# Ones beside the values: one 128-column product for values and denominators in a fused attention and feed-forward kernel

## Chip, cores, metric

One core of one Trainium2 chip. The metric is the device time of one execution in microseconds, lower is better.

## The reference, cut

```python
def _attn_ref(q, k, v):                      # 8 batches, 8 heads, 576 tokens, 64 columns
    scores = np.matmul(q, k.transpose(0, 1, 3, 2)) / sqrt(64)
    mask = np.abs(pos[:, None] - pos[None, :]) <= 32
    scores = np.where(mask, scores, -1e9)
    attn = np.exp(scores - max)
    attn = attn / (np.sum(attn, axis=-1, keepdims=True) + 1e-09)
    return np.matmul(attn, v)

x = attn_out.transpose(0, 2, 1, 3).reshape(4608, 512)
h = x @ w_in                                 # 512 -> 2048
g = 0.5 * h * (1 + tanh(c * (h + 0.044715 * h**3)))
out = g @ w_out                              # 2048 -> 512
```

## The kernel before

A turn of the main loop handles 512 tokens: 112 products of 256 columns of the second layer (a seven-product scheme for 2 x 2 blocks), and between them, by a plan, the attention of the next batch; then the first layer of the next 512 tokens. Heads go in pairs. For a pair `g` the steps are `s` (scores and their exponential), `m` (mask), `v` (weigh, and invert the sums) and `x` (spread: multiply and store into the ring `xT`). `-1` means the tails of the batch before.

```python
PLAN = {6: "s0 v-1", 24: "s1", 26: "m0", 31: "x-1", 40: "m1", 42: "v0 s2", 48: "x0", 56: "m2",
        61: "v1 s3", 64: "x1", 80: "m3", 81: "v2 s4", 88: "x2", 97: "v3", 104: "m4", 112: "x3"}
RING = 1536
...
ones = const.tile([128, 64], FP16, name="ones")
Vs = [const.tile([128, 5, H, 64], FP16, name=f"V{i}") for i in range(2)]
yp = ctx.enter_context(tc.tile_pool(name="yp", bufs=3))
psO = ctx.enter_context(tc.tile_pool(name="psO", bufs=1, space=PSUM))
...
def weigh(b, g, other=False):
    o = bank(1) if other else psO.tile([128, 512], FP32, name="ps_o", tag="O")
    d = psO.tile([128, 512], FP32, name="ps_d", tag="D")
    for i, (hf, pr, k0, c, p0, p1, off) in enumerate(todo):      # four pieces of keys
        for w, bk in ((0, o), (1, d)):
            for h in range(2):                                   # head h: 64 of the rows
                r0 = 64 * h
                nc.tensor.matmul(bk[r0:r0 + 64, ...],
                    V[:, c, 2 * pr + h, :] if w == 0 else ones,
                    pes[hf][:, h, ...], start=(i == 0), stop=(i == len(todo) - 1))
    return o, d

def invert(b, g, d):                                             # 1/d as exp(-ln d)
    nc.scalar.activation(lt[:, 0:n], d[:, 0:n], AF.Ln)
    nc.scalar.activation(lt[:, 0:n], lt[:, 0:n], AF.Exp, scale=-1.0)

def spread(b, g, o, lt):
    pos, done = b * S % RING, 0
    while done < n:                                              # two pieces where the ring wraps
        e = min(n - done, RING - pos)
        nc.vector.tensor_tensor(xT[:, g, pos:pos + e], o[:, done:done + e],
                                lt[:, done:done + e], op=ALU.mult)
        done, pos = done + e, (pos + e) % RING
```

The ring wraps in batches 2 and 5, which are made in turns 1 and 4. `ps_o` and `ps_d` are one PSUM bank each (PSUM is the on-chip memory that products are summed in; `xT`, `lt`, `pe` and `V` lie in the other one, SBUF).

The softmax here doesn't subtract the row's maximum and nothing guards it: scores larger than these inputs give would overflow.

Of the kernel before, what the change touches and what calls it, by code (L numbers as in the profile page):

```python
# [54 lines left out]
           [(t4, fc) for t4 in (2, 3) for fc in range(16)])  # L55


RING = 1536


@with_exitstack
def kernel(
# [32 lines left out]
    ap_ = ctx.enter_context(tc.tile_pool(name="ap_", bufs=2))  # L95
    gp = ctx.enter_context(tc.tile_pool(name="gp", bufs=1))
    stage = ctx.enter_context(tc.tile_pool(name="stage", bufs=5))
    yp = ctx.enter_context(tc.tile_pool(name="yp", bufs=3))
    psM = ctx.enter_context(tc.tile_pool(name="psM", bufs=1, space=PSUM))
    psS = ctx.enter_context(tc.tile_pool(name="psS", bufs=1, space=PSUM))  # L100
    psO = ctx.enter_context(tc.tile_pool(name="psO", bufs=1, space=PSUM))
# [8 lines left out]
    kinds = [MAIN[0], MAIN[1], TAIL, MAIN_0[1], TAIL_0]  # L110
    masks = [const.tile([128, width(ps)], FP16, name=f"mask{i}") for i, ps in enumerate(kinds)]
    KTs = [const.tile([128, NPAIR, 640], FP16, name=f"KT{i}") for i in range(2)]
    Vs = [const.tile([128, 5, H, 64], FP16, name=f"V{i}") for i in range(2)]
    w_in16 = big.tile([128, 4, DF], FP16, name="w_in16")
    w_out16 = big.tile([128, NF, DM], FP16, name="w_out16")
    xT = big.tile([128, NPAIR, RING], FP16, name="xT")
# [3 lines left out]
    def load_early(b):  # L120


        qr = rawp.tile([128, H, 256], FP32, name="qr")
        kr = rawp.tile([128, H, 256], FP32, name="kr")
        tr = tailp.tile([128, H, 64], FP32, name="tr", tag="tr")
        raws[b] = [qr, kr, tr]

        def qk(h0):
            for src, dst in ((q, qr), (k, kr)):
                nc.sync.dma_start(  # L130
                    dst[:, h0:h0 + 2, :],
                    src[b, h0:h0 + 2, 0:512, :].rearrange("h (p j) d -> p h (j d)", j=4))

        def vs(*heads):
            for h in heads:
                if h == 0:
                    raws[b].append(stage.tile([128, 4, H, 64], FP32, name="vr", tag="stage"))
                    raws[b].append(tailp.tile([128, H, 64], FP32, name="vt"))
                nc.sync.dma_start(raws[b][3][:, :, h, :],  # L139
                                  v[b, h, 0:512, :].rearrange("(c p) d -> p c d", p=128))  # L140

        def tails():
            nc.sync.dma_start(tr[0:64, :, :], q[b, :, 512:576, :].rearrange("h s d -> s h d"))  # L143
            nc.sync.dma_start(tr[64:128, :, :], k[b, :, 512:576, :].rearrange("h s d -> s h d"))

        def vtail():
            k0 = 448 if b else 512
            nc.sync.dma_start(raws[b][4][0:S - k0], v[b, :, k0:S, :].rearrange("h p d -> p h d"))

        return qk, tails, vs, vtail  # L150

    def load_qk(b):


        qr = rawp.tile([128, H, 256], FP32, name="qr")
        kr = rawp.tile([128, 4, H, 64], FP32, name="kr")
        qt = tailp.tile([16, H, 256], FP32, name="qt")
        kt = tailp.tile([64, H, 64], FP32, name="kt", tag="tr")
        raws[b] = (qr, kr, qt, kt)
        nc.sync.dma_start(qr, q[b, :, 0:512, :].rearrange("h (p j) d -> p h (j d)", j=4))  # L160
        for c in range(4):
            nc.sync.dma_start(kr[:, c, :, :],
                              k[b, :, 128 * c:128 * c + 128, :].rearrange("h p d -> p h d"))
        nc.sync.dma_start(qt, q[b, :, 512:576, :].rearrange("h (p j) d -> p h (j d)", j=4))
        nc.sync.dma_start(kt, k[b, :, 512:576, :].rearrange("h p d -> p h d"))

    def load_v(b):
        V = Vs[b % 2]
        for c in range(4):
            nc.gpsimd.dma_start(V[:, c, :, :],  # L170
                                v[b, :, 128 * c:128 * c + 128, :].rearrange("h p d -> p h d"))
        nc.gpsimd.dma_start(V[:, 4, :, :], v[b, :, 448:576, :].rearrange("h p d -> p h d"))

    w_in_v = moe_w_in.rearrange("(c p) f -> p c f", p=128)
    w_out_v = moe_w_out.rearrange("(c p) f -> p c f", p=128)
# [62 lines left out]
            off += 4 * n  # L238
    nc.vector.memset(ones, 1.0)
    nc.vector.memset(KTs[0][:, :, 576:640], 0.0)  # L240
    nc.vector.memset(Vs[0][64:128, 4, :, :], 0.0)

    halfs = {}
    QTs = {}
# [10 lines left out]

    def cast_vt(b):
        n = 128 if b else 64
        (nc.gpsimd.tensor_copy if b else nc.scalar.copy)(Vs[b % 2][0:n, 4, :, :], raws[b][4][0:n])

    def cast_v(b, pr):  # L260
        vr = raws[b][3]
        hs = slice(2 * pr, 2 * pr + 2)
        nc.gpsimd.tensor_copy(Vs[b % 2][:, 0:4, hs, :], vr[:, :, hs, :])  # L263


    def cast_tails(b, eng):
        t16 = hp.tile([128, H, 64], FP16, name="t16")
        eng.tensor_copy(t16, raws[b][2])
        halfs[b].append(t16)

# [31 lines left out]
    def cast_and_turn(b):  # L302
        cast_open(b)
        q16, k16 = halfs[b]
        qr, kr, qt, kt = raws[b]
        qt16 = hp.tile([16, NPAIR, 4, 2, 64], FP16, name="qt16")
        kt16 = hp.tile([64, NPAIR, 2, 64], FP16, name="kt16")
        def queries(src, dst, p0, p1):
            for pr in range(NPAIR):
                nc.vector.tensor_copy(  # L310
                    dst[:, pr, :, :, :].rearrange("p j h d -> p h j d"),
                    src[:, 2 * pr:2 * pr + 2, :].rearrange("p h (j d) -> p h j d", j=4))
            nc.sync.dma_start_transpose(QTs[b].rearrange("d r j p -> d (r j) p")[:, :, p0:p1],
                                        dst.rearrange("p r j h d -> p (r j h d)"))

        queries(qr, q16, 0, 128)
        for pr in range(NPAIR):
            nc.vector.tensor_copy(k16[:, pr, :, :, :], kr[:, :, 2 * pr:2 * pr + 2, :])
            nc.sync.dma_start_transpose(
                KTs[b % 2][:, pr, 0:512].rearrange("d (c p) -> d c p", c=4),  # L320
                k16[:, pr, :, :, :].rearrange("p c h d -> p (c h d)"))
        queries(qt, qt16, 128, 144)
        nc.vector.tensor_copy(kt16.rearrange("p r h d -> p (r h d)"), kt.rearrange("p h d -> p (h d)"))
        nc.sync.dma_start_transpose(
            KTs[b % 2][:, :, 512:576], kt16.rearrange("p r h d -> p (r h d)"))
# [38 lines left out]
    def mask(b, g, hfs=(0, 1)):  # L364
        for hf, (m, prs, pieces) in enumerate(halves_of(b, g)):
            if hf not in hfs:
# [3 lines left out]
                pe, pe, m.rearrange("p (o w) -> p o w", o=1).broadcast_to(list(pe.shape)),  # L370
                op=ALU.mult)

    def weigh(b, g, other=False):

        pes = groups.pop((b, g))
        V = Vs[b % 2]
        o = bank(1) if other else psO.tile([128, 512], FP32, name="ps_o", tag="O")
        d = psO.tile([128, 512], FP32, name="ps_d", tag="D")
        todo = [(hf,) + row for hf, (m, prs, pieces) in enumerate(halves_of(b, g))
                for row in placed(prs, pieces)]  # L380
        for i, (hf, pr, k0, c, p0, p1, off) in enumerate(todo):
            q0, n = (0, cut(b)) if g < 4 else (cut(b), 144 - cut(b))
            at = 0 if g < 4 else pr * 4 * n
            for w, bk in ((0, o), (1, d)):
                for h in range(2):
                    r0 = 64 * h
                    nc.tensor.matmul(  # L387
                        bk[r0:r0 + 64, at:at + 4 * n].rearrange(
                            "d (j p) -> d j p", j=4)[:, :, p0 - q0:p1 - q0],
                        V[:, c, 2 * pr + h, :] if w == 0 else ones,  # L390
                        pes[hf][:, h, off:off + 4 * (p1 - p0)].rearrange("k (j p) -> k j p", j=4),
                        start=(i == 0), stop=(i == len(todo) - 1), skip_group_check=True)
        return o, d
# [1 line left out]
    def size(b, g):  # L395
        return 4 * cut(b) if g < 4 else 4 * NPAIR * (144 - cut(b))

    def invert(b, g, d):
        n = size(b, g)
        lt = ap_.tile([128, 512], FP32, name="lt")  # L400
        nc.scalar.activation(lt[:, 0:n], d[:, 0:n], AF.Ln)  # L401
        nc.scalar.activation(lt[:, 0:n], lt[:, 0:n], AF.Exp, scale=-1.0)  # L402
        return lt

    def spread(b, g, o, lt):
        n = size(b, g)
        if g < 4:
            pos, done = b * S % RING, 0
            while done < n:
                e = min(n - done, RING - pos)  # L410
                nc.vector.tensor_tensor(xT[:, g, pos:pos + e], o[:, done:done + e],  # L411
                                        lt[:, done:done + e], op=ALU.mult)
                done, pos = done + e, (pos + e) % RING
        else:
            pos = (b * S + 4 * cut(b)) % RING
# [13 lines left out]
    def ffn_in(t, n, d0=0, d1=4, then=True):  # L429
# [3 lines left out]
        if d0 == 0:  # L433
# [4 lines left out]
            else:  # L438
                if t:
                    i = (first(t), 2, 1 - first(t))[n % 3] if n < NF - 1 else 2  # L440
                else:
                    i = fc if fc < 2 else (fc - 4) % 3
                phs[fc] = bank(i) if i < 2 else psO.tile([128, 512], FP32, name="ph", tag="D")
        ph = phs[fc]
        for dc in range(d0, d1):
            nc.tensor.matmul(ph, w_in16[:, dc, fc * 128:fc * 128 + 128],  # L446
# [169 lines left out]

    def weighed(g):
        o, d = weigh(0, g, other=(g % 2 == 0))
        ods[g] = (o, invert(0, g, d))

    ods = {}
    score(0, 0)
# [74 lines left out]
    for t in range(NT):  # L697
# [19 lines left out]
        for i in range(113 if t else 65):  # L717
            for act in plan.get(i, "").split():
# [22 lines left out]
                elif kind == "v":  # L741
                    bb, gg = group(g)
                    o, d = weigh(bb, gg)
                    ods[g] = (o, invert(bb, gg, d))
                    if t and g < 0 and b + 1 < B:
                        load_v(b + 1)
                    if t and g == (3 if att else -1):
                        load_table(gelu_set)
# [8 lines left out]
                ffn_out(t, i)  # L757
        if t == 0:
            load_table(gelu_set)
            load_v(2)  # L760
        else:
            ffn_last(t)
# [31 lines left out]
```

## Time and profile before

| | before |
|---|---|
| time, median (range) | 311.58 us (310.9 to 312.27) |
| start of turn 1 in the trace | 74.72 us |
| turns 1 to 7 | 32.27, 31.80, 31.80, 31.87, 31.80, 31.80, 26.66 us |
| rest | 17.2 us |
| busy: TensorE, VectorE, ScalarE | 96%, 64%, 65% |

A turn's length is read from the timeline of TensorE: from the first product of a turn's second layer to the next turn's. Turn 7 has no attention. The median is that of four runs (the prediction had three of them).

### The profile page before, as it was taken

How to read it: one execution, taken by the hardware profiler on the slowest of the kernel's cores; microseconds unless marked ns; L12 is line 12 of the kernel's file. 1: busy time of each engine (PE TensorE's matmuls, PEld its weight loads, DVE VectorE, ACT ScalarE, POOL GpSimd, SP SyncE). 2: the span in 40 equal slices, each digit the busy share in tenths (PEclk: the TensorE clock that was granted, in tenths of full speed). 3: DMA queues.
4: the chain of work that ended last, by engine and by line, in shares of the span. 5: the costliest groups of instructions: out<-in, count | busy, mean ns of one | idle time of the engine just before them, and what ended most of it. 6: DMA issues, size and time to landing. Idle time of an engine off the chain costs nothing.

```text
span 310.0 us, 6731 instructions
## 1 busy us (share of the span) xinstructions
PE 298.4 (96%) x2643; PEld 187.5 (61%) x2643; DVE 198.4 (64%) x453; ACT 200.1 (65%) x315; POOL 104.1 (34%) x158
## 2 busy tenths in 40 slices
PE   7879999999999999999999999999999999999993
PEld 3453545445784588548854785478647764784583
DVE  5663587768969477947785678666866643633451
ACT  1676576567677786768676777677768676706600
POOL 3656456093019210921094108510710061006000
PEclk9999999999999999999999999999999999999999
DMA  6999998999987998799779995999391022004013
GB/s 198 247 333 373 373 348 164 316 191 152 227 178 177 158 216 128 137 173 242 131 157 138 258 132 126 167 223 165 90 170 34 2 69 68 2 0 135 2 37 99
DMA packets 120061, 50.64 MB, mean 163 GB/s; under 512 B 101327, under 2 KB 113359, under 8 KB 120030
## 3 DMA queue, kind: packets, MB, share of 16 engines
q1 hardware_dynamic: 84329, 37.50, 57.2%
q0 software_dynamic: 34768, 11.54, 31.4%
q10 hardware_dynamic: 933, 1.18, 1.2%
q8 instruction: 20, 0.33, 0.5%
q14 instruction: 11, 0.09, 0.1%
HBM read 37.62 MB, written 9.44 MB: 152 GB/s over the span
## 4 chain that ended last, share of the span: by engine, by line
PE 78%; SPq 10%; DMA 7%; DVE 2%; issue 1%; POOL 0%; POOLq 0%
PE mm L544 31%; PE mm L446 22%; PE ph L446 13%; SPq L139 5%; PE ps_o L387 4%; PE ps_s L354 3%; DMA wst<-in_moe_w_in_dram 3%; PE ps_d L387 3%; DMA qr<-in_q_dram 3%; SPq L130 2%; DMA tr<-in_k_dram 1%; PE mm L515 1%; SPq L181 1%; SPq L143 1%; SPq L185 1%
## 5 line engine op out<-in xcount | busy, mean ns | idle before, releaser
L446 PEld LDWEIGHTS <-w_in 128*128 128x128 f16 x576 | 56.0, 98 | 66.4 <-POOL w_in L190 1.1
L446 PE MATMUL mm<-xT,w_in 128*128 128x512 f16 x352 | 86.3, 379 | 0.6 <-DVE xT L411 0.6
L506 POOL DMA_DIRECT2D out_dram<-y x77 | 45.2, 595 | 115.4 <-DVE y L573 114.7
L454 ACT ACTIVATE gT<-mm 128x512 f16<-128x512 f32 x88 | 52.4, 599 | 37.1 <-PE mm L446 37.1
L446 PE MATMUL ph<-xT,w_in 128*128 128x512 f16 x224 | 58.6, 379 | 0.2 <-POOL w_in L190 0.2
L490 DVE TENSOR_TENSOR s<-gT 128x512 f16<-128x512 f16 x64 | 26.9, 420 | 42.1 <-ACT gT L454 42.1
L544 PEld LDWEIGHTS <-s 128*128 128x128 f16 x512 | 48.6, 98 | 7.5
L360 ACT ACTIVATE pe<-ps_s 128x704 f16<-128x704 f32 x64 | 43.3, 728 | 8.8 <-PE ps_s L354 8.8
L544 PE MATMUL mm<-t,s 128*128 128x256 f16 x376 | 45.7, 273 | 0.0
L401 ACT ACTIVATE lt<-ps_d 128x480 f32<-128x480 f32 (+3 forms) x40 | 22.2, 556 | 31.1 <-PE ps_d L387 31.1
L454 ACT ACTIVATE gT<-ph 128x512 f16<-128x512 f32 x56 | 33.0, 599 | 13.0 <-PE ph L446 12.9
L544 PEld LDWEIGHTS <-gT 128*128 128x128 f16 x384 | 36.0, 98 | 7.3
L544 PE MATMUL mm<-w_out,gT 128*128 128x256 f16 x256 | 32.8, 273 | 0.0
L369 DVE TENSOR_TENSOR pe<-pe,mask 128x704 f16<-128x704 f16 x64 | 31.5, 528 | 1.9 <-ACT pe L360 1.7
L411 DVE TENSOR_TENSOR xT<-ps_o,lt 128x480 f16<-128x480 f32 (+5 forms) x38 | 20.2, 548 | 12.5 <-ACT lt L402 12.5
L387 PEld LDWEIGHTS <-V 128*64 128x64 f16 x336 | 18.1, 109 | 12.0 <-issue 5.7
L402 ACT ACTIVATE lt<-lt 128x480 f32<-128x480 f32 (+3 forms) x40 | 23.5, 587 | 1.3
L387 PE MATMUL ps_o<-pe,V 128*64 128x160 f16 (+2 forms) x244 | 21.8, 241 | 1.1 <-POOL V L263 0.8
L87 ACT ACT_TABLE_LOAD x17 | 21.8, 1283 | 1.1 <-PEq L778 0.8
L387 PE MATMUL ps_d<-pe,ones 128*64 128x192 f16 (+2 forms) x264 | 22.4, 235 | 0.0
L170 POOL DMA_DIRECT2D V<-in_v_dram x24 | 22.0, 942 | 0.0
L387 PEld LDWEIGHTS <-ones 128*64 128x64 f16 x336 | 18.6, 110 | 0.1
(77 smaller groups left out, 298.1 us busy)
## 6 DMA issues: line engine op xcount, KB each, us to landing
kr<-in_k_dram SPq DMA_DIRECT2D x32, 256.0 KB, 6.3
qr<-in_q_dram SPq DMA_DIRECT2D x6, 1024.0 KB, 7.3
V<-in_v_dram POOLq DMA_DIRECT2D x30, 128.0 KB, 8.0
wst<-in_moe_w_in_dram SPq DMA_DIRECT2D x3, 1024.0 KB, 7.9
wst<-in_moe_w_out_dram SPq DMA_DIRECT2D x3, 1024.0 KB
qr<-in_q_dram SPq DMA_DIRECT2D x8, 256.0 KB
vr<-in_v_dram SPq DMA_DIRECT2D x16, 128.0 KB, 7.6
out_dram<-y POOLq DMA_DIRECT2D x24, 48.0 KB, 2.4
```

The source lines that it names most:

```text
L87: nc.scalar.add_instruction(mybir.InstLoadActFuncSet(name=nc.get_next_instruction_name(), act_func_set_id=which, ins=[], outs=[]))
L170: nc.gpsimd.dma_start(V[:, c, :, :], v[b, :, 128 * c:128 * c + 128, :].rearrange("h p d -> p h d"))
L360: nc.scalar.activation(pe, ps[:, :, 0:w], AF.Exp, scale=SCALE)
L369: nc.vector.tensor_tensor(pe, pe, m.rearrange("p (o w) -> p o w", o=1).broadcast_to(list(pe.shape)), op=ALU.mult)
L387: nc.tensor.matmul(bk[r0:r0 + 64, at:at + 4 * n].rearrange("d (j p) -> d j p", j=4)[:, :, p0 - q0:p1 - q0], V[:, c, 2 * pr + h, :] if w == ...
L401: nc.scalar.activation(lt[:, 0:n], d[:, 0:n], AF.Ln)
L402: nc.scalar.activation(lt[:, 0:n], lt[:, 0:n], AF.Exp, scale=-1.0)
L446: nc.tensor.matmul(ph, w_in16[:, dc, fc * 128:fc * 128 + 128], xT[:, dc, t * 512 % RING:t * 512 % RING + 512], start=(dc == 0), stop=(dc = ...
L454: nc.scalar.activation(gTs[t][:, fc, :], phs[fc], AF.Gelu_apprx_tanh)
L490: nc.vector.tensor_tensor(dst, x, y, op=op)
L506: (eng or turn_about[0] if t == NT - 1 else eng or nc.gpsimd).dma_start(out_v[b, j, q0 + p:q0 + p + e, cols], yo[m:m + e, cols])
L544: nc.tensor.matmul(pys["apart"][:, 0:256] if apart else py[:, blk, :], lhsT, wino[w][:, f, :], start=(new and i % (8 if one else 16) == 0) ...
```

## The change

Intent: a pair's weigh has two products of 64 columns for values and two for denominators in each piece of keys, which side by side stream no less than two products of 128 columns. If ones lie beside each head's values, one product of 128 columns gives values and denominators of a head, in full-array mode like its neighbours, with half the instructions and no change of tiling mode. The price: in bank `o` the denominators of head 0 now lie on rows 64 to 127, in bank `d` those of head 1 on rows 0 to 63. So Ln and multiply are each issued twice, on 64 rows. It holds for all four pairs of batches 2 to 7.

```diff
+FUSED = (0, 1, 2, 3)
-    yp = ... bufs=3
+    yp = ... bufs=2
-    Vs = [const.tile([128, 5, H, 64], ...
+    Vs = [const.tile([128, 5, NPAIR, 3, 64], ...         # v0 | ones | v1
 def load_v(b):
-    for c in range(4): nc.gpsimd.dma_start(V[:, c, :, :], ...)       (and one for c = 4)
+    for c, k0 in enumerate((0, 128, 256, 384, 448)):
+        for h in range(2): nc.gpsimd.dma_start(V[:, c, :, 2 * h, :], v[b, h::2, k0:k0 + 128, :]...)
+def fused(b, g): return b > 1 and g in FUSED
 def weigh(...):
+    if fused(b, g):
+        for h, bk in enumerate((o, d)):
+            nc.tensor.matmul(bk[:, ...], V[:, c, pr, h:h + 2, :], pes[hf][:, h, ...], ...)
+        continue
 def invert(b, g, o, d):
+    if fused(b, g):
+        nc.scalar.activation(lt[0:64, 0:n], o[64:128, 0:n], AF.Ln)
+        nc.scalar.activation(lt[64:128, 0:n], d[0:64, 0:n], AF.Ln)
 def spread(b, g, o, lt, d):
-        nc.vector.tensor_tensor(xT[:, g, pos:pos + e], o[:, done:done + e], lt[:, done:done + e], ...)
+        for bk, rows in ((o, slice(0, 64)), (d, slice(64, 128))) if fused(b, g) else ((o, slice(0, 128)),):
+            nc.vector.tensor_tensor(xT[rows, g, pos:pos + e], bk[rows, done:done + e],
+                                    lt[rows, done:done + e], op=ALU.mult)
 def ffn_in(...):
+    if n == 1: i = 3            # column 1 goes to a score bank instead of bank D
```

(Cut: some small tiles share buffers to make room, casts of values skip the ones, and the ones are filled on GpSimd in turns 0 and 1.)

## The prediction

> **What bounds the kernel now.** I read the page first, then the timeline of one steady turn (107 to 139 us) engine by engine, then the instruction groups with shapes kept apart. A "turn" is one pass of the main loop: 112 products of the second layer (L544) with the next batch's attention woven in, then the first layer (L446) for the next 512 tokens.
>
> ```profile
> PE 298.4 (96%) x2643; PEld 187.5 (61%) x2643; DVE 198.4 (64%) x453; ACT 200.1 (65%) x315; POOL 104.1 (34%) x158
> PE 78%; SPq 10%; DMA 7%; DVE 2%; issue 1%; POOL 0%; POOLq 0%
> PE mm L544 31%; PE mm L446 22%; PE ph L446 13%; SPq L139 5%; PE ps_o L387 4%; PE ps_s L354 3%; DMA wst<-in_moe_w_in_dram 3%; PE ps_d L387 3%; DMA qr<-in_q_dram 3%; SPq L130 2%; DMA tr<-in_k_dram 1%; PE mm L515 1%; SPq L181 1%; SPq L143 1%; SPq L185 1%
> ```
>
> TensorE is busy 96% and holds 78% of the chain that ended last. Every microsecond put into its order is paid; the others have a third of their time free on average. The weighing products (L387), which are what changes, hold only 7% of the chain.
>
> The averages hide how close the attention steps stand. In the TensorE, ScalarE and VectorE timelines of that turn (start us, length us, engine, line):
>
> ```profile
> 111.96 1.25 PE L544 MATMUL mm<-w_out,gT 128*128 128x256 f16 x10
> 113.14 0.26 PE L387 MATMUL ps_o<-pe,V 128*64 128x160 f16 x2
> ...
> 113.69 0.22 PE L387 MATMUL ps_d<-pe,ones 128*64 128x128 f16 x2
> 113.84 0.46 PE L354 MATMUL ps_s<-QT,KT 64*128 64x160 f16 x8
> 114.24 0.83 PE L544 MATMUL mm<-w_out,gT 128*128 128x256 f16 x6
> ...
> 116.42 0.26 PE L387 MATMUL ps_o<-pe,V 128*64 128x160 f16 x2
> ```
> ```profile
> 113.95 0.57 ACT L401 ACTIVATE lt<-ps_d 128x480 f32<-128x480 f32 x1 [1.32 <-PE ps_d L387]
> 114.56 0.60 ACT L402 ACTIVATE lt<-lt 128x480 f32<-128x480 f32 x1
> 115.06 1.33 ACT L360 ACTIVATE pe<-ps_s 128x704 f16<-128x704 f32 x2
> ```
> ```profile
> 115.11 0.69 DVE L559 COPY y<-mm 128x512 f32<-128x512 f32 x1 [1.43 <-PE mm L544]
> 115.72 0.65 DVE L411 TENSOR_TENSOR xT<-ps_o,lt 128x480 f16<-128x480 f32 x1
> 116.28 0.92 DVE L369 TENSOR_TENSOR pe<-pe,mask 128x704 f16<-128x704 f16 x2
> ```
>
> Weigh, Ln, Exp, multiply is one chain, and ps_o and ps_d are single PSUM tiles, so the next weigh needs the multiply's end. Here it ends at 116.37 and the next weigh starts at 116.42: no slack. The four weighs (v0 to v3) start at 113.14, 116.42, 119.81, 122.64; the multiplies end at 116.37, 119.32, 122.52: slack 0.05, 0.49, 0.12 us. In turn 1, where the multiply came late, the wait is already there:
>
> ```profile
> 84.61 0.26 PE L387 MATMUL ps_o<-pe,V 128*64 128x160 f16 x2 [0.36 <-DVE xT L411]
> ```
>
> **What the Trainium skill says.** "TensorEngine Tiling (Array Packing)", Key Properties: changing the tiling mode drains TensorE. The trace agrees: products of 256 columns start 0.109 us apart, the tenth of the row at 111.96 starts at 112.94, so 113.05 would be next, but the 128*64 products start at 113.14, 0.09 late; the change to 64*128 costs as much (113.69 + 0.055 of streaming = 113.745 against 113.84). The same page, Restrictions: column tiling excludes the fast weight load; loads of 64 columns take 109 to 110 ns, those of 128 columns 98, so full width should not be bound by loads. The transposes at 32.09 and 32.32 (four 128-column products each, a new load for each) start 0.23 us apart, 57 ns each: agrees. "ScalarE: Activation LUTs", What ACT_TABLE_LOAD costs: 186 ns + 0.833 ns per element of the free dimension, neighbours overlapping by 93 ns. For 480 that is 586 ns; the trace has 571 and 603, and pieces of 512 start 0.49 apart. Rows do not enter: the 64x512 cast took 619 ns, the 128x512 activations 599.
>
> **The change, part by part.**
>
> Weigh. Removed: half of its instructions, 16 products and loads become 8. Not removed: streaming. Before, two 64-column products ran side by side on the two column halves (pairs start 3 ns apart). Fused, each takes the whole array. Per group 160+192+192+128 = 672 columns, twice; 69+82+82+56 ns per pass (the spacings of the pairs), so 0.58 us against 0.605. The real saving is the mode changes: one per weigh for v0 to v2 (a score follows, which still changes), two for v3. Five times 0.10 + four times 0.025 = 0.6 us a turn, 3.6 us in six turns.
>
> Inversion. Each group gets a second Ln, since denominators lie in two banks, 64 rows each, at unchanged 480 columns: 24 x 0.57 = 14 us of ScalarE work, and it is in the chain: +0.47 us with overlap.
>
> Multiply. Two instructions of 64 rows for one of 128. Rows do not help here either (16x512 casts 438 ns, 128x512 423). The second follows the first by 0.56 us (115.72 to 116.28): +0.56 in the chain.
>
> New chain, counted from a weigh's first product: last product starts 0.52, ends 0.74; Ln 0.73 (bank O is ready a product earlier), second Ln 1.20 to 1.77; Exp 1.81 to 2.41; multiplies at 2.45 and 3.02, the second ends 3.67; with 0.04 of signalling the second bank is free at 3.71. The next weigh's first product needs only O (3.15), its second needs D, so it runs as though begun at **3.64**. Stretches of a turn:
> - v0 to v1: 3.28 before. The y copy (L559) waits for the sixth L544 product after the score: weigh 0.58, change of mode 0.10, score 0.40, five spacings of 0.109, product 0.27, signal 0.04, so it starts at 1.93 and holds VectorE for 0.60 (115.11 to the next start at 115.72 is 0.61), to 2.53. The multiply starts 0.08 late: 3.72.
> - v1 to v2: 3.39, now 3.64.
> - v2 to v3: 2.83, now 3.64. (TensorE alone would be there after 0.58 + 0.10 + 0.28 for the shorter score + 16 x 0.109 = 2.70: the largest wait, 0.9.)
> - v3 to the third column of the next first layer: 4.07 before (122.64 to 126.71). Now the fourth part of columns 0 and 1 waits for the second multiply (3.71; TensorE is there at 0.58 + 15 x 0.109 + 6 x 0.216 = 3.51), then column 2, whose bank they free, waits for the L582 adds behind that multiply: they start at 3.58 and take 0.74 (the row at 125.26), so 4.33 with the signal about 4.38.
>
> Sum 15.38 against 13.57: +1.81; v0 itself starts 0.11 earlier: **+1.70 a turn**. Six turns: +10.2. In turns 1 and 4 the token ring wraps, so four multiplies instead of two: 0.13 longer per stretch (two parts take 0.63 where one takes 0.56), eight stretches: +1.0.
>
> Turn 0: output buffers go from 3 to 2, so the copy at 55.90 waits for the store issued at 51.81; the one store whose landing shows took 6.2 us, so about 58.0. VectorE then runs 2 us late; for TensorE I estimate 0.2 at the last score and 0.5 at the bank of the third column: +0.7.
>
> Beside other work: value loads become ten 64 KB transfers for five of 128 KB (0.9 us of POOL each at most, needed a turn later); two fills with ones (192 columns took 258 ns, 128 took 205, so about 1.2 us for 1280); the shared tail buffers; column 1 moved to a score bank, which avoids one further wait on D.
>
> 311.7 + 10.2 + 1.0 + 0.7 = **323.6**, said as 323.5.
>
> **The rivals.**
> (a) The gain as meant: the chain has room, only mode changes count: 311.7 - 3.6 = 308. For it: ScalarE and VectorE are a third idle. Against it: slacks of 0.05, 0.49 and 0.12 where about 1.0 is added.
> (b) Half-height instructions cost about half. Then the chain stays near its old length and the time is 308 to 312. Against it: the 16- and 64-row figures above.
> (c) The ten value transfers arrive late, or the late casts delay the transposing transfers that the first score needs. For it: in turn 1 values of batch 2 landed at 76.2 and were used at 80.9. In steady turns a wide margin (landed 117.0, used about 145). Up to +2 once: 325.
> (d) TensorE bound by full-width loads, at 98 ns each: 8 x 0.098 = 0.78 for 0.58, hidden in part in the chain: +4 more, 327. Against it: the transposes.
>
> **Range and chances.** The chain argument rests on durations of the same instructions in this trace, and its waits have almost nothing before them to absorb. Errors of 0.1 per stretch make 2.4 us, turn 0 and (c) some 2 more. Range 318 to 328. Slower by over 2% means above 318.0; only (a) or (b) or a large error of mine prevents it: 0.85 slower, 0.13 same, 0.02 faster.
>
> **What would show it.** Right: 192 products of L387 fewer (24 groups of 8 for 24 of 16); Ln rows of 64x480 at about 570 ns, multiplies of 64x480 at about 650; ps_o and ps_d products of L387 waiting 0.4 to 1 us for the multiply, about 20 such waits, largest at v3; turns of 33.5 us for 31.8. TensorE busy share falls. Wrong: half-height rows under 400 ns, no waits on xT ahead of L387, or waits on V or KT loads in their place.

## The result

| | before | after | difference |
|---|---|---|---|
| time, median of four (range) | 311.58 | 332.03 (330.63 to 332.22) | |
| start of turn 1 | 74.72 | 76.25 | +1.53 |
| turns 1 and 4 (ring wraps) | 32.27, 31.87 | 36.40, 35.88 | +4.13, +4.01 |
| turns 2, 3, 5, 6 | 31.80 each | 34.52 each | +2.72 each |
| turn 7 and rest | 43.88 | 43.78 | -0.1 |

The ratio is 1.0647, 95% interval 1.0609 to 1.0684. Ratios here and below are the mean time of one kernel's fast runs over that of the other's of the same rounds, so not quite the ratio of the quoted medians. The kernel is 20.5 us slower, where +11.9 was predicted: the direction was right and the size was not, and the time lies above the predicted range of 318 to 328.

First the page of the kernel after: busy times, then the chain that ended last by engine and by line.

```profile
PE 301.3 (91%) x2451; PEld 187.5 (57%) x2451; DVE 218.9 (66%) x485; ACT 213.3 (65%) x339; POOL 124.1 (38%) x190
PE 55%; DVE 16%; ACT 10%; DMA 8%; SPq 5%; issue 4%; POOL 1%; DVEq 0%; POOLq 0%
PE mm L474 19%; PE mm L572 16%; PE ph L474 11%; DVE xT L435 9%; ACT lt L424 4%; DMA wst<-in_moe_w_out_dram 3%; ACT lt L421 3%; ACT lt L420 3%; DMA wst<-in_moe_w_in_dram 3%; PE ps_d L396 3%; DMA out_dram<-yo 2%; PE ps_s L359 2%; PE ps_o L396 2%; SPq L134 1%; SPq L143 1%
```

Exactly the 192 products foretold are gone from TensorE, yet its share of the chain falls from 78% to 55%. What came in its place are the multiply (L435, 9%), the two Ln (L420, L421) and the Exp (L424), 10% of ScalarE together: on neither engine is the busy share above 66%. Instruction groups of the kernel after, shapes apart (busy us and mean ns of one, then the idle time ahead and who ended it):

```profile
L420 ACT ACTIVATE lt<-ps_o 64x480 f32<-64x480 f32 x24 | 13.6, 567 | 28.1 <-PE ps_o L396 28.1
L435 DVE TENSOR_TENSOR xT<-ps_d,lt 64x480 f16<-64x480 f32 x16 | 10.6, 660 | 0.5
L396 PE MATMUL ps_d<-pe,V 128*128 128x160 f16 x24 | 5.8, 240 | 6.4 <-DVE xT L435 6.3
```

Sixty-four rows cost what 128 did: 567 ns for the Ln, 660 ns for the multiply. The same plain turn (turn 2, from the first weigh on) on TensorE, by the products that start each weigh:

```profile
118.70 0.23 PE L396 MATMUL ps_o<-pe,V 128*128 128x160 f16 x1
...
122.65 0.24 PE L396 MATMUL ps_d<-pe,V 128*128 128x160 f16 x1 [0.47 <-DVE xT L435]
...
126.54 0.24 PE L396 MATMUL ps_d<-pe,V 128*128 128x160 f16 x1 [0.45 <-DVE xT L435]
...
130.43 0.24 PE L396 MATMUL ps_d<-pe,V 128*128 128x160 f16 x1 [0.47 <-DVE xT L435]
```

Each later weigh's second product waits for the second multiply. This is the wait that the prediction named. But the weighs come 3.88 to 3.89 us apart, not 3.64 to 3.72. Why shows on ScalarE and VectorE:

```profile
119.43 0.57 ACT L420 ACTIVATE lt<-ps_o 64x480 f32<-64x480 f32 x1 [1.14 <-PE ps_o L396]
120.02 0.56 ACT L421 ACTIVATE lt<-ps_d 64x480 f32<-64x480 f32 x1
120.61 0.60 ACT L424 ACTIVATE lt<-lt 128x480 f32<-128x480 f32 x1
121.12 1.33 ACT L365 ACTIVATE pe<-ps_s 128x704 f16<-128x704 f32 x2
```
```profile
120.64 0.69 DVE L587 COPY y<-mm 128x512 f32<-128x512 f32 x1 [1.30 <-PE mm L572]
121.25 0.65 DVE L435 TENSOR_TENSOR xT<-ps_o,lt 64x480 f16<-64x480 f32 x1
121.93 0.66 DVE L435 TENSOR_TENSOR xT<-ps_d,lt 64x480 f16<-64x480 f32 x1
122.62 0.93 DVE L374 TENSOR_TENSOR pe<-pe,mask 128x704 f16<-128x704 f16 x2
...
133.59 0.66 DVE L435 TENSOR_TENSOR xT<-ps_d,lt 64x480 f16<-64x480 f32 x1
134.28 0.76 DVE L610 TENSOR_TENSOR y<-mm,y 128x256 f32<-128x256 f32 x2
```

Compare the start of a row plus its length with the next start. The first multiply starts 0.61 after a copy of 0.69: they overlap by 0.08. The second multiply starts 0.68 after a first of 0.65, and the next instruction 0.69 after a second of 0.66: no overlap, on either side. The second Ln starts 0.59 after a first of 0.57, where the Exp and the exponential of scores behind it overlap by 0.09. Nothing is named as awaited there. The prediction counted 0.47 and 0.56 for these steps.

**Theory.** The mechanism was right; each 64-row instruction costs some 0.12 us more in its chain than counted, because it may not overlap its neighbours. **Rivals.** (1) Part of the loss lies outside the chain: ten value transfers, fills, the extra bank, the smaller output pool. (2) The full-width products or their loads are slower than thought. (3) The missing overlap is a dependency through the shared tile `lt` or `xT`.

### The profile page after: what moved, and what is told of

Same layout as the page of the kernel before. It is cut to its first block, busy times and chain, and to the rows that moved or that the text cites. A ratio compares the mean times of both kernels' runs of the same rounds, so it can differ in the third digit from the quotient of the medians.

```text
span 330.4 us, 6464 instructions
## 1 busy us (share of the span) xinstructions
PE 301.3 (91%) x2451; PEld 187.5 (57%) x2451; DVE 218.9 (66%) x485; ACT 213.3 (65%) x339; POOL 124.1 (38%) x190
## 4 chain that ended last, share of the span: by engine, by line
PE 55%; DVE 16%; ACT 10%; DMA 8%; SPq 5%; issue 4%; POOL 1%; DVEq 0%; POOLq 0%
PE mm L474 19%; PE mm L572 16%; PE ph L474 11%; DVE xT L435 9%; ACT lt L424 4%; DMA wst<-in_moe_w_out_dram 3%; ACT lt L421 3%; ACT lt L420 3%; DMA wst<-in_moe_w_in_dram 3%; PE ps_d L396 3%; DMA out_dram<-yo 2%; PE ps_s L359 2%; PE ps_o L396 2%; SPq L134 1%; SPq L143 1%
## 5 line engine op out<-in xcount | busy, mean ns | idle before, releaser
L175 POOL DMA_DIRECT2D V<-in_v_dram x60 | 45.2, 793 | 18.4 <-PE ps_d L405 14.2
L435 DVE TENSOR_TENSOR xT<-ps_o,lt 64x480 f16<-64x480 f32 (+6 forms) x38 | 20.8, 546 | 19.9 <-ACT lt L424 19.7
L420 ACT ACTIVATE lt<-ps_o 64x480 f32<-64x480 f32 x24 | 13.6, 567 | 28.1 <-PE ps_o L396 28.1
L396 PEld LDWEIGHTS <-V 128*128 128x128 f16 x192 | 14.9, 98 | 19.3 <-DVE xT L435 18.8
L424 ACT ACTIVATE lt<-lt 128x480 f32<-128x480 f32 (+3 forms) x40 | 23.5, 587 | 1.3
L396 PE MATMUL ps_o<-pe,V 128*128 128x160 f16 (+1 forms) x96 | 18.2, 236 | 6.0 <-DVE xT L435 5.2
L396 PE MATMUL ps_d<-pe,V 128*128 128x160 f16 (+1 forms) x96 | 16.4, 238 | 6.4 <-DVE xT L435 6.3
L359 PE MATMUL ps_s<-QT,KT 64*128 64x192 f16 (+5 forms) x336 | 17.9, 227 | 2.0 <-DVE QT L281 1.2
```

Of the source, the lines that this page charges most:

```text
L175: nc.gpsimd.dma_start(V[:, c, :, 2 * h, :], v[b, h::2, k0:k0 + 128, :].rearrange("h p d -> p h d"))
L359: nc.tensor.matmul(ps[:, h, off:off + 4 * n].rearrange("k (j p) -> k j p", j=4), KTs[b % 2][r0:r0 + 64, pr, k0:k0 + 128], QTs[b][r0:r0 + 6 ...
L396: nc.tensor.matmul(bk[:, 0:4 * n].rearrange("d (j p) -> d j p", j=4)[:, :, p0:p1], V[:, c, pr, h:h + 2, :], pes[hf][:, h, off:off + 4 * (p ...
L435: nc.vector.tensor_tensor(xT[rows, g, pos:pos + e], bk[rows, done:done + e], lt[rows, done:done + e], op=ALU.mult)
```

## Experiments

### fused_off: the change without its fused products

```diff
-FUSED = (0, 1, 2, 3)
+FUSED = ()
```

> The changed kernel with no group fused: value layout with ones, ten value transfers, two output buffers and the moved bank of column 1 stay. Theory (the loss is the longer chain weigh, two Ln, Exp, two multiplies, bank free; turn 0 apart): only the 1.7 us of turn 0 stay, 313.3 us (312.5 to 314.5). Rival (transfers, casts or the moved bank cost in every turn): 316 or more.

Measured: 314.32 us, ratio 1.009 (1.0066 to 1.0114). Turns 1 to 6 are 32.27, 31.80, 31.80, 31.87, 31.80, 31.80, to the hundredth those of the kernel before. Transfers, fills, tags and the moved bank cost nothing in any turn; rival 1 is left with turn 0. There one wait stands out (VectorE timeline of fused_off):

```profile
60.50 0.69 DVE L547 COPY yo<-mm 128x512 f32<-128x512 f32 x1 [3.41 <-DMA out_dram<-yo]
```

The third output block waits for a store to free its buffer.

### yp2: the kernel before with two output buffers

```diff
-    yp = ... bufs=3
+    yp = ... bufs=2
```

> The kernel before with two output buffers in turn 0 for three. Theory: this alone is the loss of turn 0: 313.3 us (312.6 to 314.6), VectorE's third output copy waiting 2 to 3.5 us for the store. Rival (the moved bank of column 1 or the value layout matters in turn 0): 311.5.

Measured: 314.00 us, ratio 1.0105 (1.0057 to 1.0153); turns 1 to 7 as before, turn 1 starts at 76.61. VectorE timeline of yp2:

```profile
59.35 0.69 DVE L519 COPY yo<-mm 128x512 f32<-128x512 f32 x1 [4.10 <-DMA out_dram<-yo]
```

The buffer alone gives the loss of fused_off: 2.7 us by the medians, 2.8 in fused_off, where the prediction's whole turn 0 was 0.7. How much of it is seen in one trace moves with the loads at the start: turn 1 began 1.5 us later in the trace after, 3.0 in fused_off, 1.9 here; other kernels with three buffers scatter by 0.9 below and 0.3 above the kernel before.

### halves_only: the old products, Ln and multiply cut in halves

```diff
-        nc.scalar.activation(lt[:, 0:n], d[:, 0:n], AF.Ln)
+        for rows in (slice(0, 64), slice(64, 128)) if b > 1 and g < 4 else (slice(0, 128),):
+            nc.scalar.activation(lt[rows, 0:n], d[rows, 0:n], AF.Ln)
     (the multiply likewise, on rows of xT, o and lt)
```

> The kernel before, its products untouched, with the Ln of the denominators and the multiply of batches 2 to 7 each cut into two of 64 rows. Theory: next weigh may start 4.02 us after a weigh (0.81, two Ln at 0.59, Exp 0.64, multiplies 0.68 and 0.70), stretches of 4.0, 4.0, 4.0 and 4.8 for 3.28, 3.39, 2.83 and 4.07, +3.3 a turn, +2.6 for the two wrapped turns: 334 us (329 to 337), with TensorE's instructions all as before. Rival (the full-width products or their loads cause the loss): 312 to 313.

Measured: 332.76 us, ratio 1.068 (1.066 to 1.0699). Turns: 36.73, 35.01, 35.01, 36.38, 35.01, 35.01. With the products untouched the whole loss is there, and a little more: a plain turn is +3.21 where the change makes it +2.72. So the fused products gain 0.5 us a turn, and rival 2 falls: they cost nothing. This 0.5 is not the 0.6 that the prediction counted for changes of mode and streaming: only v0 starts earlier by a saved change (0.09 us, 6.05 us into turn 2 for 6.14), and ahead of v1 to v3 TensorE waits anyway. The rest is gained in the chain, 0.11 from weigh to weigh (3.88 to 3.89 for 4.00), because the first Ln needs bank `o` alone and starts 0.74 us after the weigh's start (as counted in the table below) and not 0.81, and bank `d` is needed one product later. TensorE timeline of halves_only, the last weigh of turn 2:

```profile
129.07 0.26 PE L387 MATMUL ps_o<-pe,V 128*64 128x160 f16 x2 [1.10 <-DVE xT L413]
```

### ln_only and mul_only: one of the two cut in halves

> The kernel before with only the Ln of batches 2 to 7 cut into two of 64 rows. Theory (a lengthened chain costs only what exceeds its slack): chain 0.81 + 1.19 + 0.64 + 0.65 + 0.05 = 3.34 us from weigh to weigh, against stretches of 3.28, 3.39, 2.83: +0.6 a turn, 315 us (313.5 to 316.5). Rival (each part costs its share, additive): about a third to a half of the 21 us of both parts, 318 to 322.

> The kernel before with only the multiply of batches 2 to 7 cut into two of 64 rows. Theory: the multiply starts where it does now and ends 0.68 later, so stretches of 3.97, 3.64, 3.44 and 4.21 for 3.28, 3.39, 2.83 and 4.07, +1.7 a turn, +2.4 for the wrapped turns: 324 us (321 to 326). With ln_only this sums to well under the 21 us of both together or near it, which tells whether slack or shares count. Rival (additive in added busy time, 0.57 Ln against 0.66 multiply): 321 to 323 and ln_only 320.

The edits are the two halves of the one above. Measured: ln_only 314.83 us, ratio 1.0119 (1.0087 to 1.0151), plain turns 32.36 (+0.56), wrapped 33.44 and 32.50; mul_only 323.58, ratio 1.0389 (1.0369 to 1.0408), plain turns 33.43 (+1.63), wrapped 35.91 and 34.79. Together (halves_only) a plain turn was +3.21, more than 0.56 + 1.63 = 2.19: the slack ahead of a weigh is there once, and who comes second pays in full. There was more of it for the Ln than for the multiply. In a plain turn of ln_only one weigh waits, v3, for 0.43 us; in the kernel before, the multiply ahead of v1 started 0.55 us after the Exp's end, behind the y copy. Turn 1 is no clean measure in these two runs: its first score waited for a load of keys, 0.52 us in ln_only and 0.64 in mul_only, which stands in no other kernel's turn 1.

### by_head: the fused products, all of head 0 first

```diff
-        for i, (...) in enumerate(todo):
-            for h, bk in enumerate((o, d)):
+        for h, bk in enumerate((o, d)):
+            for i, (...) in enumerate(todo):
                 nc.tensor.matmul(...)
```

> The changed kernel with the eight products of a fused weigh ordered by head: four into the first bank, then four into the second. Theory: the first Ln starts 0.24 us earlier and the second bank is needed 0.29 instead of 0.07 us after the weigh starts, worked through a turn +0.8 instead of +2.7 us: 320 us (317 to 323), v2 to v3 stretch about 3.0 for 3.9. Rival (engine busy time or products themselves): no change, 331 to 333.

Measured: 321.45 us, ratio 1.0335 (1.0294 to 1.0377); plain turns 32.68, wrapped 35.04 and 34.01. Half of the loss goes with the order of eight products: the first Ln starts while head 1 is still streaming, and the next weigh's four products for bank `o` need only the first multiply. This supports the chain as the cause, since nothing of the work is changed. Timeline of by_head, third and last weigh:

```profile
126.83 0.45 PE L395 MATMUL ps_o<-pe,V 128*128 128x160 f16 x4
127.53 0.46 PE L395 MATMUL ps_d<-pe,V 128*128 128x160 f16 x4 [0.25 <-DVE xT L437]
```

### probe_base: is it the rows? (inconclusive)

The kernel before, with each Ln and multiply of the pairs repeated on 64 rows into the same tile: rows 0 to 63 in pairs 0 and 2, rows 64 to 127 in pairs 1 and 3.

> The kernel before with each Ln and each multiply of batches 2 to 7 followed by a harmless repeat on 64 rows: rows 0 to 63 for head pairs 0 and 2, rows 64 to 127 for pairs 1 and 3. Theory (an instruction whose first partition differs from its predecessor's does not overlap it): for pairs 0 and 2 the repeat starts 0.47 to 0.50 us after the Ln and 0.56 after the multiply, for pairs 1 and 3 0.60 and 0.68, and what follows the latter starts after its end. Rival (64-row instructions never overlap, or the second write of the same tile waits): 0.60 and 0.68 in all four. Time about 330 us, of no interest.

One run, 333.56 us. The repeats followed after 0.60 (Ln) and 0.69 (multiply) in all four pairs: writing the tile that the first had just written, they had been given a wait for it. That hid the question, though on VectorE the next instruction overlapped a repeat on rows 0 to 63 (0.58 us after the start of one of 0.65) and not one on rows 64 to 127 (0.69 after one of 0.66). On ScalarE the Exp behind had a wait too, and came after 0.60 in all four.

### probe_apart: the same repeats into scratch tiles of their own

```diff
+        if b > 1 and g < 4:
+            rows = slice(64 * (g % 2), 64 * (g % 2) + 64)
+            nc.scalar.activation(scr[0][rows, 0:n], d[rows, 0:n], AF.Ln)
     (and a multiply of those rows into scr[1]; output buffers 2, to make room)
```

> The kernel before with each Ln and each multiply of batches 2 to 7 followed by a repeat on 64 rows that writes a scratch tile of its own: rows 0 to 63 for pairs 0 and 2, rows 64 to 127 for pairs 1 and 3. No write is shared, so no wait between them. Theory (first partition differs from the predecessor's: no overlap): for pairs 0 and 2 the repeat starts 0.47 to 0.50 us after the Ln and 0.56 after the multiply and the next instruction overlaps it; for pairs 1 and 3 0.60 and 0.68 and the next one starts after its end. Rival (half-height instructions never overlap): the same in all four pairs, 0.60 and 0.68. The time is of no interest.

One run, 330.73 us, of which only the spacings count. Ln to its repeat: 0.47 us on rows 0 to 63 (pairs 0 and 2), 0.60 on rows 64 to 127. Multiply to its repeat: 0.56 and 0.58 against 0.68 and 0.69. No wait stands between, and no tile is shared in writing. Rival 3 falls, and so does "half height" as such: it is where the rows start (the runs here compare starts at rows 0 and 64 only). ScalarE timeline of probe_apart, pair 1 (Ln, repeat on rows 64 to 127, Exp, exponential of scores):

```profile
122.36 0.57 ACT L403 ACTIVATE lt<-ps_d 128x480 f32<-128x480 f32 x1 [1.10 <-PE ps_d L389]
122.96 0.57 ACT L406 ACTIVATE scr<-ps_d 64x480 f16<-64x480 f32 x1
123.55 0.60 ACT L407 ACTIVATE lt<-lt 128x480 f32<-128x480 f32 x1
124.17 1.35 ACT L362 ACTIVATE pe<-ps_s 128x704 f16<-128x704 f32 x2
```

One thing did not fit my wording "an instruction on rows 64 to 127 overlaps neither neighbour": the Exp and the exponential at 124.17, both on all 128 rows, did not overlap either (0.62 apart; 0.49 in pair 0).

That led me back to the Trainium skill, to a section that I had not read when I predicted. "VectorE: DVE Perf Modes", section "Two Vector instructions with no wait between them", gives a rule, there for VectorE: an instruction is held until every earlier one has finished if the 32-row quadrant in which an input starts is not that of the last instruction that read the same memory (SBUF or PSUM, each by itself), or if its output starts in another quadrant than the last output into that memory. If ScalarE does the same, 124.17 is explained: PSUM had last been read at rows 64 up, by the repeat, and the Exp between reads SBUF alone.

### probe_memory: reads and writes set apart

```diff
+        if b in (3, 4, 6, 7) and g < 4:
+            up, low = slice(64, 128), slice(0, 64)
+            src, dst = (up, low) if g % 2 == 0 else (low, up)
+            nc.scalar.activation(scr[0][dst, 0:n], d[src, 0:n], AF.Ln)
     (and nc.vector.tensor_copy(scr[1][dst, 0:n], o[src, 0:n]) behind the multiply;
      in batches 2 and 5 the multiply in halves, both pieces of a half before the other half)
```

> Kernel before, output buffers 2; spacings in the trace count, not the total. (1) Batches 3, 4, 6, 7: behind each Ln a second Ln of 64 rows, behind each multiply a copy of 64 rows, into scratch: in pairs 0 and 2 from PSUM rows 64 to 127 to SBUF rows 0 to 63, in pairs 1 and 3 the reverse. (2) Batches 2 and 5 (wrapped ring): multiply in halves, both pieces of rows 0 to 63 first, then both of 64 to 127. Theory M (the Trainium skill, 'VectorE: DVE Perf Modes', 'Two Vector instructions with no wait between them', taken to hold for ScalarE too: held if the first quadrant read in, or written to, a memory is not that of the last instruction that read, or wrote, that memory). ScalarE, pairs 0 and 2: Ln to probe held, 0.59 us; probe to Exp 0.46; Exp to the next exponential of scores, which reads PSUM, held, 0.61. Pairs 1 and 3: 0.59, 0.59, then 0.50. VectorE, pair 0: copy held, about 0.67; copy to mask, which touches no PSUM, overlapped; the y instruction behind, which reads PSUM, held. Pair 1: copy held and the y add behind it held. Four wrapped multiplies 1.45 us for 1.66 in alternating order; turns 1 and 4 35.3 and 34.2 for 35.91 and 34.79. Rival 1 (rows from 64 up on either side: no overlap with either neighbour): probe to Exp 0.59 and copy to mask not overlapped everywhere, Exp to exponential 0.50. Rival 2 (written rows alone count): pairs 0 and 2 all overlapped, 0.47, 0.46, 0.50.

One run, 329.35 us, spacings only. ScalarE timeline of probe_memory, pair 0 (reads PSUM at row 64, writes SBUF at row 0), then pair 1 (the reverse):

```profile
117.00 0.57 ACT L403 ACTIVATE lt<-ps_d 128x480 f32<-128x480 f32 x1 [1.31 <-PE ps_d L389]
117.59 0.57 ACT L407 ACTIVATE scr<-ps_d 64x480 f16<-64x480 f32 x1
118.06 0.59 ACT L408 ACTIVATE lt<-lt 128x480 f32<-128x480 f32 x1
118.68 1.35 ACT L362 ACTIVATE pe<-ps_s 128x704 f16<-128x704 f32 x2
...
120.97 0.57 ACT L403 ACTIVATE lt<-ps_d 128x480 f32<-128x480 f32 x1 [0.94 <-PE ps_d L389]
121.56 0.56 ACT L407 ACTIVATE scr<-ps_d 64x480 f16<-64x480 f32 x1
122.15 0.60 ACT L408 ACTIVATE lt<-lt 128x480 f32<-128x480 f32 x1
122.66 1.33 ACT L362 ACTIVATE pe<-ps_s 128x704 f16<-128x704 f32 x2
```

Pair 0: probe held (0.59), Exp, which touches no PSUM, not held (0.47), the next reader of PSUM held (0.62). Pair 1: probe held (0.59), Exp held because it writes SBUF at row 0 again (0.59), the next reader of PSUM not held (0.51). All six are as the rule has them memory by memory, and so in all four batches of the trace; both rivals named in the expectation fall. For ScalarE this tests reads of PSUM and writes to SBUF; the other two were not varied. On VectorE the copy came 0.68 and 0.69 behind the multiply, the mask in pair 0, which reads no PSUM, only 0.58 behind a copy of 0.66 (not held), the y add in pair 1 0.69 behind one of 0.65 (held): as expected too.

The wrapped multiplies, four per group, first of mul_only (order of rows low, up, low, up), then of probe_memory (low, low, up, up), each a line of the VectorE timeline of turn 1:

```profile
83.64 1.66 DVE L412 TENSOR_TENSOR xT<-ps_o,lt 64x384 f16<-64x384 f32 x4
```
```profile
84.78 1.45 DVE L421 TENSOR_TENSOR xT<-ps_o,lt 64x384 f16<-64x384 f32 x4
```

The same four instructions, two changes of quadrant fewer: 0.21 us less. Turn 4 fell from 34.79 to 33.98, which is 4 x 0.21 within 0.03, and turn 1 from 35.91 to 34.39, where 0.6 was expected. Of this fall 0.64 is not the order but the wait for keys named above, which probe_memory does not have (TensorE timeline of mul_only):

```profile
75.27 0.46 PE L354 MATMUL ps_s<-QT,KT 64*128 64x160 f16 x8 [0.64 <-DMA KT<-k]
```

### all_retimed, two_fused, plain_retimed: can the idea be made to pay?

All three have the by_head order, three output buffers again (paid for by a single `lt` buffer) and a plan that starts the steps earlier where TensorE has room. all_retimed fuses all pairs, two_fused pairs 1 and 2, plain_retimed none, with the plan of two_fused.

```diff
-FUSED = (0, 1, 2, 3)
+FUSED = (1, 2)                    # all_retimed: (0, 1, 2, 3); plain_retimed: ()
-PLAN = {6: "s0 v-1", 24: "s1", ...}
+PLAN = {6: "s0 v-1", 21: "m0", 25: "s1", 28: "x-1", 32: "v0 s2", 42: "m1", 43: "x0", 48: "v1 s3",
+        54: "m2", 56: "x1", 73: "v2", 75: "m3", 90: "x2", 102: "s4 v3", 104: "m4", 112: "x3"}
+# all_retimed: {6: "s0 v-1", 21: "m0", 26: "s1", 31: "x-1", 33: "v0", 36: "s2", 37: "m1", 41: "x0", 45: "m2",
+#   53: "v1 x1", 64: "s3", 69: "m3", 71: "v2", 73: "x2", 76: "s4", 92: "v3", 94: "m4", 112: "x3"}
-    yp = ... bufs=2
+    yp = ... bufs=3
-        lt = ap_.tile(...)            # pool of 2
+        lt = tailp.tile(...)          # pool of 1
```

> All four groups fused, products ordered by head, three output buffers in turn 0 (paid for by one buffer of inverses), and the attention steps moved within the turn (weighs at products 33, 53, 71, 92 for 42, 61, 81, 97) so that each chain has room. Theory, a turn worked through with the durations of the traces: +0.4 us a turn and no loss in turn 0, 314 us (312 to 316). Rival (something other than waits for the chain costs): stays near by_head's 321 less the 2 to 3 us of turn 0, 318 to 319.

> Only head pairs 1 and 2 fused, ordered by head, weighs at products 32, 48, 73, 102 and the last score just ahead of the last weigh, three output buffers. Theory: the mode changes of two weighs are saved (0.10 and 0.2 us a turn, the second because no score follows) and no weigh waits: -0.3 us a turn, 309.7 us (308.5 to 311). Rival (the fused chain cannot be hidden): 311.5 or more.

> The same plan and buffers as two_fused with no group fused: the control. Theory: moving the steps alone gains nothing, 311.5 us (311 to 312.5). Rival (the plan, not the fusing, makes the difference): as two_fused.

| | median us | ratio (95%) | plain turn | turns 1, 4 |
|---|---|---|---|---|
| before, same rounds | 311.49 | 1 | 31.80 | 32.27, 31.87 |
| all_retimed | 314.41 | 1.0088 (1.0067 to 1.0109) | 31.75 | 34.57, 32.94 |
| two_fused | 310.38 | 0.9959 (0.9935 to 0.9983) | 31.54 | 32.95, 31.56 |
| plain_retimed | 312.71 | 1.0026 (1.0 to 1.0052) | 31.89 | 33.11, 31.90 |

With room in the plan the fused plain turn is just under the old one. That is not how all_retimed's 314 was forecast (+0.4 us a turn): turns 1 and 4 lose the 3.4 us, while the plain turns gain. Two pairs fused beat both kernels, by 0.4% of the kernel before: real by the interval, but small. Its control, the same plan unfused, is no faster than before (312.71, just above the 311 to 312.5 expected), so the gain is the fusion's: 31.89 - 31.54 = 0.35 us a turn. That fits three changes of mode at 0.10 and two weighs that stream 0.025 faster, with the prediction's own figures (pair 1 saves the change on entry, since a score follows; pair 2 those on entry and exit); neither kernel has a wait of over 0.08 us on TensorE in turn 2 that could hide or make it.

In two_fused the wrap no longer costs: turn 4 is 31.56 for 31.87. What it loses in turn 1, 0.68 us, is the plan's: v0 was moved up to product 32, and in turn 1 alone VectorE also forms two differences of weights (L509, 1.22 us each), one of them ahead of the multiply of the tails. The control has the same wait, of 1.07, and all_retimed one of 0.95. TensorE timeline of two_fused:

```profile
80.49 0.26 PE L406 MATMUL ps_o<-pe,V 128*64 128x160 f16 x2 [1.06 <-DVE xT L442]
```

## Why the prediction was right and wrong

**Right.** What binds: the chain weigh, Ln, Exp, multiply, bank free, next weigh, with too little slack to absorb the additions; halves_only shows it by giving the loss without the change's products. Half-height instructions at full length: 567 and 660 ns. Full-width products not bound by loads: a weigh takes 0.58 us as forecast. The price of a change of mode fits the 0.35 of two_fused against its control; that halves_only also gives some 0.5, near the 0.6 forecast, is chance, since most of it comes from the chain. Transfers of values harmless: fused_off. The waits stand where they were foretold, 23 ahead of L396 for the multiply where about 20 were said, and the 192 products are gone.

**Wrong, and by which terms.** The failed step is the cost of the added instructions: "+0.47 us with overlap" for the second Ln and "The second follows the first by 0.56 us" for the multiply. They were read from neighbours that start at row 0. Measured: 0.59 and 0.68, because a change of the starting quadrant forbids the overlap, at 0.12 each, and a third time behind the last multiply, where the adds (L610) followed at 0.69 and not 0.56. By stretches of a plain turn (a weigh's start is taken as that of its second product, the one that waits, less the 0.07 between the two products where nothing waits):

| stretch | before | forecast | after | missed | holds that make it |
|---|---|---|---|---|---|
| v0 to v1 | 3.28 | 3.72 | 3.88 | 0.16 | multiply 0.12; Ln 0.12 less the 0.08 that the copy had delayed anyway |
| v1 to v2 | 3.39 | 3.64 | 3.89 | 0.25 | Ln 0.12, multiply 0.12 |
| v2 to v3 | 2.83 | 3.64 | 3.89 | 0.25 | Ln 0.12, multiply 0.12 |
| v3 to the third column | 4.07 | 4.38 | 4.73 | 0.35 | Ln 0.12, multiply 0.12, adds 0.13 |

That is 1.01 a turn, of which the holds make 1.01 (0.16 + 0.24 + 0.24 + 0.37; so close by the luck of rounding), over six turns 6.1 us. This split is arithmetic on the spacings: no run takes the holds alone out of a plain turn, as probe_memory does with some of the wrapped ones. The second mis-sized term is the wrapped ring, "0.13 longer per stretch": four multiplies that alternate between the halves are held at every step. Turns 1 and 4 lost 1.41 and 1.29 more than plain ones, 2.7 against 1.0 forecast: 1.7 us; probe_memory recovers 0.2 per group by reordering. The third is turn 0: 1.5 in this trace against 0.7, the store's landing being 1 us later than read from the one landing in the trace before, plus some scatter of the start. Forecast 11.9 + 6.1 + 1.7 + 0.8 = 20.5.

**The range** failed with it: "Errors of 0.1 per stretch make 2.4 us" allowed for errors of 0.1 where the same systematic 0.12 entered two or three times in each stretch. And the rule was to be had: it stands in a page that I had not looked up, since I looked at pages for the operations added (ScalarE, tiling) and not for what their row ranges do on VectorE.

What stays open: why the hardware holds in this way (the rule is a model that fits), and whether the held steps could be avoided altogether, by a layout in which both halves' denominators lie on the rows of their values.

## What to carry to other kernels

Splitting an elementwise step by rows costs a whole second instruction, and if the halves start in different quadrants, the overlap with both neighbours besides: count it from two neighbouring lines of a trace whose operands start at the same partitions, and order pieces so that equal starts follow each other. Before saving work on the busiest engine, look at the slack of the chain that feeds it back: here 0.05 to 0.49 us of slack ahead of the weighs met 0.59 + 0.68 us of added latency, and what TensorE saved could not show. If such a change is wanted, give the chain room in the plan first, and measure the new plan without the change as well.

## What the Trainium skill lacked or had wrong

- "ScalarE: Activation LUTs" (What ACT_TABLE_LOAD costs) says that ACTIVATEs back to back overlap by about 93 ns, without a condition. Here 0.47 us apart at 0.57 long (overlap 0.10) when the starting quadrants agree, 0.58 to 0.59 when they do not (none). ScalarE follows the rule that "VectorE: DVE Perf Modes" (Two Vector instructions with no wait between them) gives for VectorE, reads of PSUM and writes to SBUF each judged by itself: all six spacings in probe_memory. No page says so for ScalarE.
- That VectorE section has the rule, and the trace agrees, but gives no price: 0.66 to 0.69 us for 0.56 to 0.58 between multiplies of 480 columns, so about 0.11 us for each held instruction, and again for the one behind it that goes back to the first quadrant.
- That fewer rows do not shorten an instruction is not said on the ScalarE page, whose formula is for 128 rows: 64 x 480 took 562 to 567 ns and 128 x 480 took 571, where the formula gives an estimate of 586.
- "TensorEngine Tiling (Array Packing)" (Key Properties) names the drain at a change of mode without a figure: about 0.10 us each, and 0.35 us a turn for three of them and two weighs' streaming (two_fused against plain_retimed).
